# Linear attention's numerators computed transposed in strips of 512 tokens, with denominators written out 16-fold through DRAM, one-sided scaling of the queries' features, and half of the query tiles placed beside the keys

## The chip, the cores and the metric

The kernel runs on one core of one Trainium2 chip. The time is device time in microseconds (us) of one execution. Engines are named as in the profile: PE is TensorE (PEld its weight loads), DVE is VectorE, ACT is ScalarE, POOL is GpSimd, and SP is the engine that issues most of the DMAs.

## What is computed

One transformer block over 2048 tokens of width 512: a linear attention with 32 heads of 16 features, whose queries and keys go through a learned map and two softmaxes, then a mixture of 8 experts, all of them used for every token.

```python
def _A_ref(x, wqkv, w_phi, wo):                 # S = 2048, D = 512, H = 32, Dh = 16
    qkv = ... (x @ wqkv) ...
    pq = jnp.einsum("bhsd,hdf->bhsf", q, w_phi)
    pk = jnp.einsum("bhsd,hdf->bhsf", k, w_phi)
    phi_q = jnp.concatenate([_softmax(pq), _softmax(-pq)], axis=-1)
    phi_k = jnp.concatenate([_softmax(pk), _softmax(-pk)], axis=-1)
    kv = jnp.einsum("bhsf,bhsd->bhfd", phi_k, v)
    z  = jnp.einsum("bhsf->bhf", phi_k)
    num = jnp.einsum("bhqf,bhfd->bhqd", phi_q, kv)
    den = jnp.einsum("bhqf,bhf->bhq", phi_q, z)[..., None] + 1e-6
    o = num / den
    return ...(o)... @ wo
def _B_ref(x, wg, w1, w2):                      # E = 8, F = 1792, top 8 of 8
    h = _gelu(jnp.einsum("nd,edf->nef", xt, w1))
    y = jnp.einsum("nef,efd->ned", h, w2)
    out = jnp.einsum("ne,ned->nd", cw, y)       # cw: softmax of xt @ wg, renormalized
h = x + _A_ref(_layernorm(x), A_wqkv, A_w_phi, A_wo)
out = h + _B_ref(_layernorm(h), B_wg, B_w1, B_w2)
```

## The kernel before

The tokens are 16 tiles of 128; four tiles are a chunk of 512, two chunks a half. Every large product is made of three fast matmuls of 512 columns (`mm3`, lines 73 to 75), on operands that `split` (lines 62 and 63) has cut into a high part (a copy on ACT) and a low part (a subtraction on DVE). Matmuls on plain 32-bit data, as those of `k_sum`, `q_num` and `gate`, are issued as two instructions each.

**Attention.** For each tile of x: `x_norm`, `x_trans`, `x_low` make its transposed operand; `k_proj` makes keys and values; `k_exp` and `k_feat` make the keys' features; `k_sum` (line 264) adds 32 small products to `kvp`, a PSUM bank that is held through all keys and has, for each head, 32 features by 16 values plus one column of sums. When the last tile is in, `keys_done` spreads it into `kv` (line 307) with zeros where the heads don't match (`hmask`). Queries follow tile by tile: `q_proj`; `q_sub` (lines 202 and 203 on DVE, 282 and 283 on POOL); `q_exp` (line 287); `q_feat`, which is `feat_norm` (sums on line 209, reciprocals on 210, one product over all 1024 features on POOL, line 211); `q_trans` (eight 128x128 transposes, line 299, two copies by ACT, line 300); `q_num` (eight matmuls of 68 columns, line 319, that take the transposed features as stationary weights, then on DVE the denominator plus 1e-6 on 323, its reciprocal on 324, the quotient on 325, twice each); `q_otrans` (four transposes of the result, and its split); `q_out` (twelve fast matmuls with `wos`, the residual added on 338, the layer norm's statistics); `q_norm` (line 182), `q_ntrans` (line 189 and the copies on 355). For each chunk `gate` (line 370), `gate_norm` and `gate_rows` (lines 401 to 406) make the expert weights.

**Experts.** `moe` runs over experts and blocks of F for the first half of the tokens, then the second. `quad` makes seven products of six fast matmuls each (two-by-two block products with seven multiplications), `down` seven more, whose sums go to DRAM by accumulating DMAs on POOL's queue (line 602). `operands(0)` cuts the first half into seven operand blocks; `spill(1)` writes the second half's to DRAM, with `block_sums` making the differences on line 419.

**What sets the order.** `steps` calls the stages in the order of `STAGES`, each with a lag in steps; a scheduling layer then fixes one static order for each engine. Engines run their queue in order, so an instruction that waits holds up all behind it. PSUM has eight banks: four of the pool `ps`, four of `pacc` (one is `kvp` until the keys are done). Tiles in SBUF come from two pools with 43 and 15 slots, handed out in turn. Four of the 16 query projections stand ahead of the last `k_sum`; all other query work on PE comes behind it, and its end overlaps with the first quads.

## Time and profile before

| | before |
|---|---|
| median of 3 runs | 2330.6 us (2330.36 to 2331.09) |
| the profiled execution's own time | 2329.5 us |
| span of its profile | 2327.8 us |
| PE, DVE, ACT, POOL busy | 99%, 92%, 76%, 22% of the span |
| first matmul of a key projection | 13.39 us |
| last instruction of the last `k_sum` begins | about 133 us |
| first matmul of the experts (line 622) | 260.76 us |

The profile lists groups of instructions by source line, engine and tile names, with their count, their busy time and the mean duration of one. PE's instructions overlap in its pipeline, so a group's pace, the distance from one to the next, is less than the mean duration of one. In the view of stretches, the idle time of an engine is the length less its busy time; PEclk is the granted clock. Tiles of both SBUF pools are called s.

### The profile page before, as it was taken

The page shows a single profiled execution, that of the slowest core. Times are in us where ns is not written, and L with a number is a line of the kernel's source. Part 1 is how long each engine was busy: PE and PEld are TensorE (multiplying, and loading weights), DVE is VectorE, ACT ScalarE, POOL GpSimd, SP SyncE. Part 2 cuts the span into 40 slices and gives each one's busy share as a digit, 9 for nine tenths or more (in the row PEclk, how much of TensorE's full clock was granted, in tenths as well). Part 3 has the DMA queues.
Part 4 walks back from the last instruction along what each step waited for, and adds up shares of the span by engine and source line. Part 5 has one row for each costly group of instructions (what it writes and reads, how often), then busy time and mean ns, then how long its engine had stood idle before and what let it go on. Part 6 is the DMA issues. An engine that isn't in the chain of part 4 may idle for free.

```text
span 2327.8 us, 34005 instructions
## 1 busy us (share of the span) xinstructions
PE 2313.0 (99%) x12100; PEld 2021.0 (87%) x12100; DVE 2135.0 (92%) x3199; ACT 1762.7 (76%) x2933; POOL 520.0 (22%) x619
## 2 busy tenths in 40 slices
PE   9999999999999999999999999999999999999999
PEld 8888888888888888888888888888888888888887
DVE  7777899999999999999998999889999999999998
ACT  5444688787777878778777887777777778777774
POOL 5576201111111111111111331211111111111121
PEclk9999999999999999999999999999999999999999
DMA  3002458888888788887889898998888888878888
GB/s 129 24 6 74 139 175 179 165 159 164 166 165 168 152 175 153 179 163 147 175 155 222 180 207 165 215 208 171 160 166 159 168 165 158 174 150 178 164 162 188
DMA packets 173497, 370.92 MB, mean 159 GB/s; under 512 B 15216, under 2 KB 80368, under 8 KB 173296
## 3 DMA queue, kind: packets, MB, share of 16 engines
q0 software_dynamic: 63776, 210.79, 54.3%
q1 hardware_dynamic: 108224, 157.77, 21.3%
q8 instruction: 96, 1.57, 0.3%
q14 instruction: 73, 0.60, 0.1%
q10 hardware_dynamic: 1328, 0.18, 0.0%
HBM read 157.34 MB, written 220.79 MB: 162 GB/s over the span
## 4 chain that ended last, share of the span: by engine, by line
PE 75%; issue 5%; DVE 4%; ACT 1%; POOL 1%; DMA 1%; POOLq 0%; DVEq 0%; ACTq 0%
PE ps L73 13%; PE ps L74 13%; PE ps L75 13%; PE pacc L74 12%; PE pacc L75 12%; PE pacc L73 12%; DVE s L63 2%; POOL acc1m L602 1%; DVE s L612 1%; DMA acc1m<-s 1%; DVE s L561 1%; ACT s L62 1%; DVE s L550 0%; DMA h<-s 0%; DVE s L419 0%
## 5 line engine op out<-in xcount | busy, mean ns | idle before, releaser
L63 DVE TENSOR_TENSOR s<-s,s 128x512 fp32r<-128x512 f32 (+1 forms) x806 | 760.9, 957 | 85.9 <-ACT s L62 77.7
L62 ACT ACTIVATE s<-s 128x512 fp32r<-128x512 f32 (+1 forms) x806 | 675.4, 844 | 14.1 <-DVE s L561 6.0
L73 PE MATMUL pacc<-s,s 128*128 128x512 f32 x1728 | 657.8, 381 | 2.6 <-DVE s L63 1.7
L74 PE MATMUL pacc<-s,s 128*128 128x512 f32 x1728 | 655.3, 379 | 0.4 <-DVE s L63 0.4
L75 PE MATMUL pacc<-s,s 128*128 128x512 f32 x1728 | 654.9, 379 | 0.0
L73 PE MATMUL ps<-s,s 128*128 128x512 f32 x1664 | 634.2, 381 | 1.5 <-ACT ps L616 0.7
L74 PE MATMUL ps<-s,s 128*128 128x512 f32 x1664 | 631.8, 380 | 0.6 <-DVE s L63 0.6
L75 PE MATMUL ps<-s,s 128*128 128x512 f32 x1664 | 631.1, 379 | 0.0
L600 ACT ACTIVATE s<-pacc 128x512 f32<-128x512 f32 x756 | 441.4, 593 | 138.7 <-PE pacc L75 134.3
L611 ACT ACTIVATE ps<-ps 128x512 f32<-128x512 f32 x448 | 257.5, 585 | 171.6 <-DVE ps L663 116.1
L73 PEld LDWEIGHTS pacc<-s,s 128*128 128x128 f32 x1728 | 326.5, 189 | 50.5 <-DVE s L63 1.5
L74 PEld LDWEIGHTS pacc<-s,s 128*128 128x128 f32 x1728 | 326.6, 189 | 47.1 <-DVE s L63 1.5
L75 PEld LDWEIGHTS pacc<-s,s 128*128 128x128 f32 x1728 | 326.6, 189 | 46.2
L73 PEld LDWEIGHTS ps<-s,s 128*128 128x128 f32 x1664 | 314.8, 189 | 50.0 <-ACT ps L616 1.6
L74 PEld LDWEIGHTS ps<-s,s 128*128 128x128 f32 x1664 | 314.8, 189 | 44.9 <-DVE s L63 1.3
L75 PEld LDWEIGHTS ps<-s,s 128*128 128x128 f32 x1664 | 314.8, 189 | 44.5
L602 POOL DMA_DIRECT2D acc0m<-s x189 | 162.2, 858 | 810.6 <-ACT s L600 790.2
L612 DVE TENSOR_TENSOR s<-ps,s 128x512 f32<-128x512 f32 x448 | 302.5, 684 | 40.0 <-ACT ps L611 33.5
L602 POOL DMA_DIRECT2D acc1m<-s x175 | 149.7, 857 | 726.2 <-ACT s L600 706.1
L561 DVE TENSOR_TENSOR s<-s,s 128x1024 f32<-128x1024 f32 x224 | 272.1, 1216 | 0.1
L616 ACT ACTIVATE ps<-ps 128x512 f32<-128x512 f32 x226 | 133.3, 590 | 53.1 <-PE ps L75 52.3
L533 DVE TENSOR_TENSOR s<-s,s 128x1024 fp32r<-128x1024 f32 x111 | 134.8, 1214 | 0.0
(121 smaller groups left out, 1774.8 us busy)
## 6 DMA issues: line engine op xcount, KB each, us to landing
acc0m<-s POOLq DMA_DIRECT2D x196, 512.0 KB, 5.7
acc1m<-s POOLq DMA_DIRECT2D x184, 512.0 KB, 5.7
s<-in_B_w_dram SPq DMA_DIRECT2D x224, 256.0 KB
s<-in_B_w_dram SPq DMA_DIRECT2D x111, 512.0 KB
s<-in_A_x_dram SPq DMA_DIRECT2D x32, 256.0 KB
s<-cwT SPq DMA_DIRECT2D x16, 512.0 KB
h<-s SPq DMA_DIRECT2D x16, 256.0 KB
acc0m<-acc0m POOLq DMA_DIRECT2D x28, 128.0 KB, 7.6
```

Source lines behind the costliest of these rows:

```text
L62: nc.scalar.activation(hi, src, AF.Copy)
L63: return eng.tensor_tensor(lo, src, hi.bitcast(F32), op=ALU.subtract)
L73: nc.tensor.matmul(out_, al, bh, start=first, stop=False, skip_group_check=True)
L74: nc.tensor.matmul(out_, ah, bl, start=False, stop=False, skip_group_check=True)
L75: nc.tensor.matmul(out_, ah, bh, start=False, stop=last, skip_group_check=True)
L533: nc.vector.tensor_tensor(sl, s, sh.bitcast(F32), op=ALU.subtract)
L561: nc.vector.tensor_tensor(r, B[a], B[b], op=ALU.subtract)
L600: nc.scalar.activation(e[:, d], p[d], AF.Copy)
L602: return nc.gpsimd.dma_start(macc[h, m], e, accum_op=ALU.add)
L611: nc.scalar.activation(src, src, AF.Gelu_apprx_tanh)
L612: nc.vector.tensor_tensor(B[b][:, q % 2], src, CW[h, e][:, int(b[2]) - 1], op=ALU.mult)
L616: nc.scalar.activation(dst, src, AF.Copy)
```

## The change

Numerators are computed transposed: the stationary operand is now a small block of `kv` (64 features of two heads by 32 values), the moving one the transposed features of 128 tokens, and the result is a strip with features on partitions and 512 tokens in a row, so that no transposes of `o` are needed ahead of `q_out`. For each chunk `q_den` makes the 32 denominators of its 512 tokens in one bank, takes their reciprocals, writes each 16 times to DRAM (`rden`), and reads them back as two tiles in the shape of the strips; `q_num` multiplies. `wo` is loaded with its rows in the strips' order (`load_wo`, 16 DMAs). `q_feat` leaves the first softmax unscaled and multiplies the second by the ratio of both sums, since a common factor of numerator and denominator drops out (1e-6 is added to the first softmax's rows of z). The differences of `spill` go to POOL. Stages are now listed with the steps at which their tiles run: query tiles 0 to 7 go beside the keys from step 6 on, 8 to 15 behind them; `q_out`, `q_norm` and `q_ntrans` run in pairs of tiles from step 22 on.

```diff
-    hmask = consts.tile([P, HG], F32, name="hmask")
...
+    rden = [dram.tile([H, Dh, TC, P], F32, name=f"rden{c}") for c in range(NT // TC)]
...
     def q_feat(t):
-        st["qf", t] = feat_norm(st.pop(("qe", t)))
+        e = st["qf", t] = st.pop(("qe", t))
+        s = work.tile([P, H, 2], F32, name="s")
+        nc.vector.tensor_reduce(s..., e..., axis=AX.X, op=ALU.add)
+        nc.vector.reciprocal(s[:, :, 1], s[:, :, 1])
+        nc.vector.tensor_tensor(s[:, :, 1], s[:, :, 0], s[:, :, 1], op=ALU.mult)
+        nc.gpsimd.tensor_tensor(e[:, :, 1, :], e[:, :, 1, :], s[:, :, 1:2].to_broadcast([P, H, Dh]), op=ALU.mult)
...
     def keys_done():
-        for g in range(NG):
-            nc.vector.tensor_tensor(kv[:, g, :]..., kvp[...]..., hmask..., op=ALU.mult)
+        for j in range(HG):
+            ...
+            nc.vector.tensor_scalar(z[r, a:...:H + 2], v[r, :, Dh], eps[r], None, op0=ALU.add)
+            nc.scalar.activation(kvn[r, :, e, :], v[r, :, :Dh], AF.Copy)
+    def q_den(c):
+        p = ps()
+        for g in range(NG):
+            for j in range(TC):
+                nc.tensor.matmul(p[j * H:(j + 1) * H, :P], zs[:, g, :], st["ph", c * TC + j][:, g, :],
+                                 start=(g == 0), stop=(g == NG - 1), skip_group_check=True)
+        d = work.tile([P, P], F32, name="den", bufs=1)
+        nc.vector.reciprocal(d, p[:, :P])
+        for j in range(TC):
+            nc.sync.dma_start(rden[c][:, :, j, :],
+                              d[j * H:(j + 1) * H].rearrange("h (o t) -> h o t", o=1).to_broadcast([H, Dh, P]))
+        for a in range(2):
+            r = st["d", c, a] = s4([P, 2, 512])
+            nc.sync.dma_start(r, rden[c][...]...)
-    def q_num(t):
+    def q_num(c):
-                nc.tensor.matmul(p[:, i * HN:(i + 1) * HN], phT[:, b * n + i, :], kv[:, b * n + i, :],
-                                 start=True, stop=True)
-            nc.vector.tensor_scalar(den, nv[:, :, Dh:], 1e-6, None, op0=ALU.add)
-            nc.vector.reciprocal(den, den)
-            nc.vector.tensor_tensor(o[...]..., nv[:, :, :Dh], den.to_broadcast([P, H // 2, Dh]), op=ALU.mult)
-    def q_otrans(t):
-        p = transposed(st.pop(("o", t)), ps_acc())
-        split(o[:, 0], o[:, 1], p)
+        for l in range(2):
+            p = [ps() for _ in range(2)]
+            for j in range(TC):
+                for g in range(KD):
+                    for a in range(2):
+                        r = slice(a * 2 * F2, (a + 1) * 2 * F2)
+                        nc.tensor.matmul(p[a][g * F2:(g + 1) * F2, j * P:(j + 1) * P], kvn[r, l * KD + g]...,
+                                         ph[j][r, l * KD + g, :], start=True, stop=True, skip_group_check=True)
+            for a in range(2):
+                r = st["d", c, a][:, l]
+                nc.vector.tensor_tensor(r, p[a], r, op=ALU.mult)
+                o = st["O", c, 2 * a + l] = s4([P, 2, 512], F32R)
+                split(o[:, 0], o[:, 1], r)
...
-        return block_sums(h, lambda b, src: nc.sync.dma_start(later[h, b], src))
+        return block_sums(h, lambda b, src: nc.sync.dma_start(later[h, b], src), nc.gpsimd)
...
+    BO = 22
+    early = [6 + t for t in range(8)]
+    STAGES = [..., (q_num, listed([21, 22, 25, 27])), ..., (q_den, listed([19, 20, 23, 25])),
+              (q_out, pairs(BO)), ...,
+              (q_proj, queries(0, [17, 17, 18, 18, 19, 19, 20, 20])), ...]
```

Three places show what the scheduler made of it. The first is PE in the middle of the query stage, one tile's numerators before, whose weights are the tile's transposed features (s_2184) and whose moving operand is kv (s_120):

```order
L75 MATMUL ps<-s_752,s_1165 128x512
L189 MATMUL pacc<-ident,s_2097 128x128 x4
L319 MATMUL ps<-s_120,s_2184 128x68 x8
L299 MATMUL pacc<-ident,s_2064 128x128 x8
L73 MATMUL pacc<-s_1889,s_2158 128x512
```

Now, at the numerators of chunk 0 (tiles s_1613 to s_1939 are transposed features, s_127 holds kv and z), with the transposes of tile 8 (line 312) and the numerators of chunk 1 (s_2004 to s_2285) right behind:

```order
L355 MATMUL ps<-s_1735,s_127 32x128 x4
L355 MATMUL ps<-s_1613,s_127 32x128 x4
L355 MATMUL ps<-s_1735,s_127 32x128 x4
L355 MATMUL ps<-s_1837,s_127 32x128 x8
L355 MATMUL ps<-s_1939,s_127 32x128 x8
L312 MATMUL ps<-ident,s_2178 128x128 x8
L355 MATMUL ps<-s_2004,s_127 32x128 x4
L355 MATMUL ps<-s_2092,s_127 32x128 x4
L355 MATMUL ps<-s_2181,s_127 32x128
L355 MATMUL ps<-s_2004,s_127 32x128 x4
```

Eight matmuls of a tile have become 64 of a chunk, which fill all four ps banks, and the transposes behind them need one of these banks again. The second place is DVE there. Before, a query tile's quotient stood among that tile's own work:

```order
L323 TENSOR_SCALAR den<-ps 128x16
L63 TENSOR_TENSOR s_2158<-pacc,s_2158 128x512
L324 RECIPROCAL den<-den 128x16
L323 TENSOR_SCALAR den<-ps 128x16
L325 TENSOR_TENSOR s_2165<-ps,den 128x256
L324 RECIPROCAL den<-den 128x16
L325 TENSOR_TENSOR s_2165<-ps,den 128x256
```

Now the first product with chunk 0's reciprocals (line 361, s_2233) stands behind the sums of two later tiles' features (line 300) and chunk 1's reciprocals (line 338):

```order
L300 TENSOR_REDUCE s<-s_2271 128x64
L300 TENSOR_REDUCE s<-s_2277 128x64
L338 RECIPROCAL den<-ps 128x128
L301 RECIPROCAL s<-s 128x32 x2
L302 TENSOR_TENSOR s<-s 128x32
L361 TENSOR_TENSOR s_2233<-ps,s_2233 128x512
L302 TENSOR_TENSOR s<-s 128x32
L361 TENSOR_TENSOR s_2235<-ps,s_2235 128x512
L361 TENSOR_TENSOR s_2233<-ps,s_2233 128x512
L361 TENSOR_TENSOR s_2235<-ps,s_2235 128x512
```

The quotient has moved behind work of other tiles. The third place is where the experts begin. Before, PE went from a query tile's output projection to one transposed tile, the priming matmuls of line 622 and the first product; DVE had made that product's low part (s_3005) among the query work:

```order
L324 RECIPROCAL den<-den 128x16
L392 RECIPROCAL gr<-gr 128x4
L325 TENSOR_TENSOR s_2927<-ps,den 128x256
L393 TENSOR_TENSOR cw<-gate,gr 128x4x8
L63 TENSOR_TENSOR s_3005<-s_2504,s_3004 128x1024
L338 TENSOR_TENSOR s_2791<-pacc,s_2791 128x512
```

Now DVE goes from the residual of tile 11 (s_3009) through the first expert weights (lines 546 to 563, the old 516 to 533) to chunk 3's four strips (s_3067 and s_3069), with the first product's low part (s_3245) among them:

```order
L187 TENSOR_SCALAR mb<-mv 128x1
L546 TENSOR_TENSOR s_3227<-s_2917 128x256
L548 TENSOR_TENSOR s_3227<-s_2917 128x256
L547 TENSOR_TENSOR s_3227<-s_3227,s_2917 128x256
L549 TENSOR_TENSOR s_3227<-s_2917,s_3227 128x256
L556 TENSOR_TENSOR s_3232<-s_2917,s_3232 128x512
L361 TENSOR_TENSOR s_3067<-ps,s_3067 128x512
L563 TENSOR_TENSOR s_3241<-s_3227,s_3240 128x1024
L361 TENSOR_TENSOR s_3069<-ps,s_3069 128x512
L63 TENSOR_TENSOR s_3245<-s_2906,s_3244 128x1024
L361 TENSOR_TENSOR s_3067<-ps,s_3067 128x512
L63 TENSOR_TENSOR s_3283<-s_3067,s_3283 128x512
```

and PE, from the last matmul of tile 11's output projection to the first of tile 12's (which reads s_3283), has little between:

```order
L75 MATMUL pacc<-s_2084,s_3000 128x512
L201 MATMUL pacc<-ident,s_3129 128x128 x4
L201 MATMUL pacc<-ident,s_3131 128x128 x4
L431 MATMUL pacc<-ident,cw 128x128
L652 MATMUL ps<-s_3244,s_3232 128x512 x2
L73 MATMUL ps<-s_3244,s_3232 128x512
L74 MATMUL ps<-s_3245,s_3232 128x512
L75 MATMUL ps<-s_3244,s_3232 128x512
L73 MATMUL pacc<-s_1798,s_3283 128x512
```

More of the change, by code (lines that the diff above doesn't have):

```diff
@@ new lines, in block_kernel, with keys_done @@
+    kz = s2([P, 2, NG, H])
+    nc.gpsimd.memset(kz, 0.0)
+    kvn, zs = kz[:, 0].rearrange("p g (e d) -> p g e d", e=2), kz[:, 1]
+    def keys_done():
+        v = kvp[:, :NG * DE].rearrange("p (g d) -> p g d", g=NG)
+        z = zs.rearrange("p g h -> p (g h)")
+        for j in range(HG):
+            s_, e = divmod(j, 2)
+            r = slice(j * F2, (j + 1) * F2)
+            a = s_ * (H // 2) + e
+            nc.vector.tensor_scalar(z[r, a:a + (NG - 1) * (H + 2) + 1:H + 2], v[r, :, Dh], eps[r], None, op0=ALU.add)
+            nc.scalar.activation(kvn[r, :, e, :], v[r, :, :Dh], AF.Copy)
@@ L337, in q_out @@
+    def q_out(t):
+        c, j = divmod(t, TC)
+        p = ps_acc()
+        for k in range(KD):
+            o = st["O", c, k]
+            mm3(p, (o[:, 0, j * P:(j + 1) * P], o[:, 1, j * P:(j + 1) * P]), wos[k], k == 0, k == KD - 1)
+            if j == TC - 1:
+                del st["O", c, k]
         r = st["h", t] = st.pop(("r", t))
@@ L989, in block_kernel @@
     wv = split_all(raw_v)
-    steps(0, 32 + NT, NT, STAGES, hook)
+    steps(0, BO + 14, STAGES, hook)
     for _ in late["m"]:
```

141 lines of the change are left out of this document (73 added, 68 removed).

## Prediction

> **What bounds the kernel now.** I read the page first: how busy each engine is, and the slices.
>
> ```profile
> span 2327.8 us, 34005 instructions
> ...
> PE 2313.0 (99%) x12100; PEld 2021.0 (87%) x12100; DVE 2135.0 (92%) x3199; ACT 1762.7 (76%) x2933; POOL 520.0 (22%) x619
> ```
>
> A busy share of 99% says only that PE nearly always has an instruction in flight. Whether it runs at its pace is seen from the starts of its matmuls, in the timeline of PE, in which two fast matmuls that are 20 apart stand here:
>
> ```profile
> 20.39 0.38 PE L73 MATMUL pacc<-s,s 128*128 128x512 f32 x1
> ...
> 24.70 0.38 PE L75 MATMUL pacc<-s,s 128*128 128x512 f32 x1
> ```
>
> (24.70 - 20.39) / 20 gives 0.216 us each. The view of stretches then shows where PE lost time: the keys (13.39 to 113.69 us), the queries, the start of the experts, and a piece of their steady run.
>
> ```profile
> 13.39:113.69 100.30, 100.13 (x1236) 86.35 (x1234) 82.66 (x150) 53.35 (x83) 56.46 (x69) 1.00 0.14 46
> 113.69:260.76 147.07, 142.52 (x1177) 127.50 (x1176) 119.54 (x286) 74.49 (x127) 88.29 (x81) 0.99 0.19 57
> 260.76:340.72 79.96, 77.87 (x421) 64.44 (x419) 73.90 (x134) 63.95 (x113) 7.49 (x16) 1.00 0.47 167
> 460.00:1000.00 540.00, 540.00 (x2504) 472.86 (x2503) 505.93 (x716) 429.58 (x717) 88.95 (x105) 1.00 0.83 165
> ```
>
> The columns are length, PE, PEld, DVE, ACT, POOL, granted clock, DMA share, GB/s. In the steady run PE is never idle: nothing there is touched, and no later wait can absorb a gain. So what the change takes out of PE's queue before about 340 us comes off the end, and each new wait of PE there goes on top. PE idled 147.07 - 142.52 = 4.6 us beside the queries and 2.1 us at the experts' start, where DVE was busy 73.9 of 80 us. There is one more loss:
>
> ```profile
> 152.60 1.08 PE L319 MATMUL ps<-s,s 128*128 128x68 f32 x8 [1.49 <-DVE s L325]
> ...
> 155.32 0.63 PE L74 MATMUL ps<-s,s 128*128 128x512 f32 x1
> 155.75 0.63 PE L75 MATMUL ps<-s,s 128*128 128x512 f32 x1
> ...
> 150.00:155.00 5.00, 3.50 (x25) 3.40 (x26) 4.96 (x12) 3.04 (x5) 3.47 (x3) 0.89 0.02 3
> 155.00:160.00 5.00, 5.00 (x26) 4.32 (x26) 5.00 (x12) 2.74 (x4) 3.42 (x3) 0.77 0.00 0
> ```
>
> After an idle 1.49 us the clock falls: fast matmuls are 0.43 us apart, half speed. From the means 0.89 and 0.77 of two stretches of 5 us, (0.11 + 0.23) x 5 x 2 = 3.4 us ran so, which costs 1.7 us. Idle and clock together are 8.4 us.
>
> **What goes from PE.** In the timeline, a query tile's old numerators and the transposes of its result:
>
> ```profile
> 172.54 0.60 PE L189 MATMUL pacc<-ident,s 128*128 128x128 f32 x4
> 172.98 1.90 PE L319 MATMUL ps<-s,s 128*128 128x68 f32 x16
> 174.72 1.04 PE L299 MATMUL pacc<-ident,s 128*128 128x128 f32 x8
> ```
>
> From start to start the transposes take 0.44 us and the 16 instructions 1.74 us (0.109 each). Over 16 tiles that is 7.0 + 27.8 = 34.8 us. The eight transposes of the features stay.
>
> **What is added on PE.** A chunk's denominators are 32 matmuls, so 64 instructions, in the form of the expert gate: 32 columns of weights, 128 moving, four column groups in turn. Its timeline:
>
> ```profile
> 227.78 1.30 PE L370 MATMUL pacc<-s,wg_raw 128*32 128x128 f32 x32
> 229.00 0.66 PE L189 MATMUL pacc<-ident,s 128*128 128x128 f32 x4
> 229.49 0.30 PE L380 MATMUL pacc<-ident,gT 128*128 128x128 f32 x1
> ```
>
> 1.22 us for 32, or 0.038 each: 2.44 us a chunk, 9.8 us in all. The numerators are 64 matmuls (128 instructions) a chunk, 512 in all, of 64 partitions by 32 columns. No row has that form. If the two row halves also run side by side, each costs half a gate's, 0.019 (9.8 us); if they don't, 0.038 (19.7 us); if nothing overlaps, line 319's 0.109 (55.8 us). I take 0.0235, 12 us, near the lower end, because consecutive matmuls alternate between the halves and between two banks. The Trainium skill, TensorE: Matmul & The Clock Gate, Part 3 on packing, has three column tiles at 2.38-fold and three by three at 6.32-fold; my estimate by that ratio for two row halves is 11 us, one less in the sum; no run here shows it. So PE's work falls by 34.8 - 9.8 - 12 = 13.0 us (bounds 15.2 and 5.3, without overlap a rise of 30.8).
>
> Packed groups also cost at their edges: the transposes behind the gate take 0.49 us to the next start, not 0.44. A dozen new groups with two edges each are 1.2 us; I take 1.5 (0 to 3).
>
> **What moves.** Eight projections (2.6 us each) and most transposes of early tiles now stand among the keys. PE's sum doesn't change by that, as long as the other engines keep up. The first stretch holds 15 key tiles: 6.7 us of PE a step, 9.3 with a projection; DVE 82.66 / 15 = 5.5, POOL 3.8. A query tile adds, from these rows:
>
> ```profile
> L209 DVE TENSOR_REDUCE s<-s 128x64 f32<-128x1024 f32 x32 | 38.8, 1213 | 22.6 <-ACT s L254 22.0 <-ACT s L287 0.7
> L202 DVE TENSOR_REDUCE mx<-s 128x32 f32<-128x512 f32 x32 | 21.3, 665 | 20.3 <-POOL s L283 20.3
> L210 DVE RECIPROCAL s<-s 128x64 f32<-128x64 f32 x32 | 17.5, 546 | 0.3
> L211 POOL TENSOR_TENSOR s<-s,s 128x1024 f32<-128x1024 f32 x32 | 63.0, 1968 | 69.7 <-DVE s L210 36.0 <-DVE mb L175 21.2 <-DVE den L323 5.6
> L282 POOL TENSOR_TENSOR s<-s,mx 128x512 f32<-128x512 f32 x16 | 18.3, 1143 | 0.0
> ```
>
> on DVE 1.2 for the sums, two extrema at 0.67 and about 0.4 for half the reciprocals and the ratio, so 2.9, which makes 8.4 of 9.3; on POOL two subtractions (2.3) and half of line 211 (1.0), in all 7.1. Both fit: PE hides them at no cost; if waits between the two engines use that slack up, I price it at 0.3 us for each of eight steps, 2.4 us. POOL also takes the four spill differences (8 us at line 211's size); behind them on its queue stand only the first accumulating DMAs, which wait for ACT anyway, and on SP the weight loads two quads ahead.
>
> **The denominators' round trip.** A chunk is 1 MB out in 2048 pieces of 512 bytes, then 1 MB back. SP must wait for the write before it issues the read. The nearest landings:
>
> ```profile
> acc0m<-s POOLq DMA_DIRECT2D x196, 512.0 KB, 5.7
> q1 hardware_dynamic: 108224, 157.77, 21.3%
> ```
>
> Two transfers at 5.7 us give 11.4. From the second row a packet takes 21.3% of 16 x 2327.8 us / 108224 = 73 ns, so 2048 over 16 engines would take 9.3 us, and by bytes 3.3; the trip lies between some 8 and 18 us. I take 11.5. The matmuls of the numerators don't wait for it, only DVE's product, and the next user of the PSUM bank.
>
> **New waits of PE**, by the order shown ahead.
> (a) The first denominators stand 0.8 us of transposes behind the last `k_sum`, and need DVE's four additions: 1 us.
> (b) Rows for ACT's copies and exponentials:
>
> ```profile
> L300 ACT ACTIVATE s<-pacc 128x512 f32<-128x512 f32 x32 | 17.9, 597 | 9.6 <-PE pacc L299 9.6
> L287 ACT ACTIVATE s<-s 128x1024 f32<-128x1024 f32 x16 | 16.9, 1058 | 40.4 <-POOL s L283 40.4
> ```
>
> Chunk 0's product stands on DVE behind tile 10's sums, whose exponentials stand on ACT behind the copy of the last early-issued projection. From that projection's end: ACT 0.6 + 1.2 + 2.1 (copies, two exponentials of 1.06), DVE 1.2 (sums), 1.1 (128 reciprocals, twice line 210), 0.6 (small ones) and 0.7 (product), so 7.5 us until a bank is free. PE has 29 denominators' matmuls (2.2 us) and 48 to 64 numerators' (about 3 us) until then, and waits 2 to 3; again 1 to 2 for the following banks. Chunk 1 repeats it behind its round trip and eight POOL subtractions of 1.14 us: 3 to 5. Of 6 to 10, I take 6.
> (c) Chunk 3. The durations:
>
> ```profile
> L338 DVE TENSOR_TENSOR s<-pacc,s 128x512 f32<-128x512 f32 x16 | 10.9, 682 | 0.3 <-PE pacc L75 0.2
> L172 DVE BATCH_NORM_STATS2 bn<-s 128x6 f32<-128x512 f32 x32 | 21.4, 670 | 3.8 <-DMA s<-in_A_x_dram 3.8
> L533 DVE TENSOR_TENSOR s<-s,s 128x1024 fp32r<-128x1024 f32 x111 | 134.8, 1214 | 0.0
> L516 DVE TENSOR_TENSOR s<-s 128x256 f32<-128x256 f32 x111 | 46.1, 415 | 0.0
> L63 DVE TENSOR_TENSOR s<-s,s 128x1024 fp32r<-128x1024 f32 x406 | 496.1, 1222 | 77.4 <-ACT s L62 72.7
> ```
>
> From tile 11's last matmul DVE has a residual and statistics (0.7 + 0.7 + 0.4), the weights' sums (4 x 0.42 + 0.7), three products (2.1), two long operations (2.4) and one short (0.7): 9.4 us, or 8.3 at the spacing of a busy DVE. PE has 2.1 us to do meanwhile: about 6 us idle, and 1.5 more until the fourth strip is split. I take 7. After so long a wait I count one clock drop, 1.7. The Trainium skill, TensorE: Matmul & The Clock Gate, Part 1, lets the clock fall only after an idle window of about 3.4 us; the trace shows half speed after 1.49 us, so the trace decides, and (b) can drop the clock too. By that rule the sum is as it stands, by the trace up to 1.7 more.
> Chunk 2 has some 20 us of PE work beside its trip: nothing.
> Sum of new waits 1 + 6 + 7 + 1.7 = 15.7, in place of the old 8.4.
>
> **DVE's relief.**
>
> ```profile
> L325 DVE TENSOR_TENSOR s<-ps,den 128x256 f32<-128x256 f32 x32 | 13.1, 418 | 0.3
> L324 DVE RECIPROCAL den<-den 128x16 f32<-128x16 f32 x32 | 7.3, 237 | 0.0
> L323 DVE TENSOR_SCALAR den<-ps 128x16 f32<-128x16 f32 x32 | 4.2, 137 | 0.0
> ```
>
> The tile's quotient leaves (twice 0.14 + 0.24 + 0.42, 1.6 us), a product of 0.68 comes, and four long differences go to POOL; where the experts start, DVE bounds PE, so I give back 1.5 of the 2.1 us idle there.
>
> **Sum.** -13.0 + 1.5 + 15.7 - 8.4 - 1.5 = -5.7 us against the profiled execution's 2329.5 (span 2327.8 and 1.7 around it): 2323.8. The median shown is 1.1 higher than that execution, so 2325 us.
>
> **Rivals.**
> - *Same*: the waits eat it. With (b) at 10, (c) at 8 and a second clock drop, the sum is +1 us, 2332. For it: (c) follows from a fixed order, DVE can't be earlier. Against: DVE loses 16 x 0.9 us of work in all. Chance 0.28, with all that falls within 0.2% (4.7 us, about what this kernel's measurement can tell from no change).
> - *Slower, by packing*: the row halves don't overlap. The point from which it decides is 0.035 us for one of the 512 instructions (17.7 us, no gain left), and from 0.044 it is slower by over 0.2%; at 0.109 the time is 2325 + 44 = 2369. For it: no row shows the form. Against: the gate's instructions, in four column groups, start 0.038 us apart, a third of line 319's distance. Chance 0.06.
> - *Slower, by the trip*: at 18 us a round trip chunk 1's product waits 6.5 us more and chunk 3's 5, for PE too: 2336. It decides from 13 to 14 us, where the trip outlasts DVE's own queue. Chance 0.16.
> - *Larger gain*: 0.019 each and waits (b) of 3 us only: 2325 - 2 - 3 = 2320, without the clock drop and (c) at 5, 2316. It is part of faster.
> - *It doesn't do what it says*: the waits only move into the keys, because POOL and DVE there, at 76 and 90%, lag behind: + 2.4 us, inside same.
>
> **Numbers.** Forecast: faster, 0.50 (2308 to 2326). Same 0.28, slower 0.22. The range from 2309 to 2338 leaves out the unpacked case and a little at the fast end.
>
> **What would show it.** Right: the group of line 355 on PE 10 to 14 us busy, that of line 335 about 10; no transposes of `o`; PE idle some 7 us between the last output projection of chunk 2 and the first of chunk 3, released by DVE line 63; idle of transposes on line 312 released by DVE line 361; the steady run unchanged. Wrong: line 355 above 20 us, DVE waits on DMA ahead of line 361, idle PE among the keys, or a steady run with another pace.

## The result: 23.5 us slower

| | median, us | ratio to before | 95% interval |
|---|---|---|---|
| before (4 runs of this comparison) | 2330.7 | 1 | |
| changed | 2354.2 | 1.0103 | 1.0085 to 1.0120 |

The forecast was 2325 us, and the range ended at 2338. The profiled execution of the changed kernel has a span of 2354.3 us, 26.5 more than before's.

The page of the changed kernel, and then its view of stretches, with the columns and the four stretches of the prediction:

```profile
span 2354.3 us, 34893 instructions
...
PE 2311.7 (98%) x12548; PEld 2008.0 (85%) x12548; DVE 2133.1 (91%) x3131; ACT 1766.9 (75%) x2937; POOL 515.0 (22%) x627
```

```profile
13.39:113.69 100.30, 100.14 (x1111) 86.16 (x1110) 80.88 (x158) 57.48 (x86) 63.90 (x77) 1.00 0.14 46
113.69:260.76 147.07, 126.58 (x1702) 105.43 (x1700) 104.75 (x198) 66.83 (x117) 63.95 (x72) 0.96 0.38 115
260.76:340.72 79.96, 67.07 (x346) 52.52 (x347) 65.50 (x114) 53.05 (x95) 15.97 (x15) 0.85 0.37 126
460.00:1000.00 540.00, 540.00 (x2504) 472.86 (x2503) 505.37 (x716) 428.63 (x715) 89.69 (x105) 1.00 0.80 164
```

The keys and the steady run are as they were: PE has no idle time there. All of the loss lies between 113.69 and 340.72 us. There PE idled 20.5 + 12.9 = 33.4 us, against 4.6 + 2.1 = 6.7 before. The clock column went from 0.99 and 1.00 to 0.96 and 0.85; (1 - clock) x length gives 5.9 + 12.0 = 17.9 us at most (some of it falls on idle time), against 1.5 by the same reckoning before. Idle time alone is 26.7 us more, as much as the span grew. PE's busy time is nearly the same (2311.7 us, 2313.0 before): what PE has less to do and what the lower clock costs it about cancel.

Where PE waited, by the view of its waits over the whole run (who waited on what for whom; sum in us, times, longest):

```profile
PE ps L335 <- DVE s L328: 5.5, 1, 5.5
PE ps L73 <- ACT ps L646: 4.4, 2, 3.9
PE ps L652 <- DVE s L563: 4.2, 1, 4.2
PE pacc L431 <- DVE cw L427: 3.9, 2, 3.6
PE pacc L73 <- DVE s L63: 3.6, 3, 2.0
PE ps L312 <- DVE s L361: 3.5, 2, 3.0
PE ps L73 <- DVE s L563: 1.8, 1, 1.8
...
PE pacc L407 <- ACT s L395: 1.3, 1, 1.3
PE ps L355 <- DVE den L338: 1.2, 1, 1.2
PE ps L73 <- DVE s L361: 0.9, 1, 0.9
...
PE ps L335 <- DVE s L361: 0.7, 1, 0.7
PE ps L73 <- ACT s L284: 0.7, 1, 0.7
PE ps L355 <- ACT s L284: 0.7, 1, 0.7
```

No single wait does it. The forecast's places are there (lines 335, 63, 312 and 355; line 652 is the experts' first product, which stands ahead of chunk 3's projections), and so is one for which a gain was forecast: lines 646, 431 and 407 and the wait of line 73 for line 563 belong to the experts' start. Of line 63's 3.6 us, 3.0 (two waits) lie in these stretches.

The first row in the timeline of PE, with what follows it:

```profile
164.75 3.64 PE L335 MATMUL ps<-s,s 128*32 128x128 f32 x64 [5.50 <-DVE s L328]
168.32 0.80 PE L73 MATMUL ps<-s,s 128*128 128x512 f32 x1
168.91 0.63 PE L74 MATMUL ps<-s,s 128*128 128x512 f32 x1
169.34 0.43 PE L75 MATMUL ps<-s,s 128*128 128x512 f32 x1
```

After 5.5 us without work the 64 instructions take 3.57 us to the next start, and fast matmuls are 0.43 us apart (169.34 - 168.91): half speed again, after this wait as after the 1.49 us of the kernel before. It does not follow every wait, though. In the same timeline:

```profile
194.33 0.48 PE L73 MATMUL pacc<-s,s 128*128 128x512 f32 x1 [2.01 <-DVE s L63]
194.65 0.38 PE L74 MATMUL pacc<-s,s 128*128 128x512 f32 x1
194.87 0.38 PE L75 MATMUL pacc<-s,s 128*128 128x512 f32 x1
```

After an idle 2.01 us, longer than 1.49, these start 0.22 us apart, at full speed. So the length of one wait doesn't settle it, and what does these runs don't show.

### The profile page after: what moved, and what is told of

The parts are those of the page before. It is cut to its first block, busy times and chain, and to the rows that moved or that the text cites. A ratio compares the mean times of both kernels' runs of the same rounds, so it can differ in the third digit from the quotient of the medians.

```text
span 2354.3 us, 34893 instructions
## 1 busy us (share of the span) xinstructions
PE 2311.7 (98%) x12548; PEld 2008.0 (85%) x12548; DVE 2133.1 (91%) x3131; ACT 1766.9 (75%) x2937; POOL 515.0 (22%) x627
## 4 chain that ended last, share of the span: by engine, by line
PE 83%; issue 6%; DVE 5%; DMA 2%; POOL 2%; ACT 2%; SPq 0%; POOLq 0%; DVEq 0%; ACTq 0%
PE pacc L73 14%; PE pacc L74 14%; PE pacc L75 14%; PE ps L73 13%; PE ps L74 13%; PE ps L75 13%; DVE s L63 2%; POOL acc1m L632 1%; DMA h<-s 1%; ACT s L62 1%; DVE s L580 0%; DVE s L591 0%; DMA acc1m<-s 0%; DVE s L642 0%; DVE s L300 0%
## 5 line engine op out<-in xcount | busy, mean ns | idle before, releaser
L63 DVE TENSOR_TENSOR s<-s,s 128x1024 fp32r<-128x1024 f32 (+1 forms) x822 | 773.7, 955 | 93.7 <-ACT s L62 83.9
L62 ACT ACTIVATE s<-s 128x1024 fp32r<-128x1024 f32 (+1 forms) x822 | 684.9, 839 | 21.8 <-DVE s L361 8.9
```

Of the source, the lines that this page charges most:

```text
L62: nc.scalar.activation(hi, src, AF.Copy)
L63: return eng.tensor_tensor(lo, src, hi.bitcast(F32), op=ALU.subtract)
```

## Experiments

Four theories stood at first. **A**: the schedule took away the query work that covered PE's waits. **E**: the denominators' trip through memory sets the waits. **C**: the packed matmuls themselves pull the clock down. **D**: POOL's differences hold DVE up. **F**, the order in the engines' queues, came in after the first four runs. (Some expectations use the letter A, or B, for the reading that stands against the one under test; each says which.) In each diff lines of the changed kernel carry a minus, unless something else is said, and `...` stands for lines left out. e4, e12 and e15 leave out the division by the denominators: they show what costs time and do not compute the block.

| run | what | median, us | ratio, 95% interval |
|---|---|---|---|
| e1_old_order | new arithmetic, old schedule (output side two steps later) | 2360.5 | 1.0131 (1.0115 to 1.0146) |
| e2_fill | idle matmuls in PE's waits | 2357.6 | 1.0117 (1.0100 to 1.0134) |
| e3_spill_dve | differences on DVE | 2350.2 | 1.0086 (1.0071 to 1.0101) |
| e4_no_trip | product reads rows of x | 2336.5 | 1.0028 (1.0017 to 1.0038) |
| e5_order_exp | exponentials ahead on ACT | 2347.5 | 1.0076 (1.0059 to 1.0093) |
| e6_read16 | written once, read 16-fold | 2343.2 | 1.0058 (1.0043 to 1.0073) |
| e7_last_sum_first | last key sums ahead | 2350.3 | 1.0087 (1.0072 to 1.0102) |
| e8_all_four | e3, e5, e6, e7 together, one transfer for the write | 2338.4 | 1.0032 (1.0020 to 1.0044) |
| e9_fill_half | e2 with half the matmuls | 2350.7 | 1.0087 (1.0070 to 1.0103) |
| b1_scaling | before + one-sided scaling | 2324.4 | 0.9975 (0.9965 to 0.9985) |
| b2_spill_pool | before + differences on POOL | 2336.7 | 1.0028 (1.0018 to 1.0038) |
| b3_scaling_early | b1 + the changed schedule | 2334.1 | 1.0018 (1.0008 to 1.0027) |
| e10_old_order_short | e1 + short trip, e3 | 2338.5 | 1.0036 (1.0023 to 1.0049) |
| e11_old_order_step | e10 + one step of slack | 2339.8 | 1.0039 (1.0024 to 1.0054) |
| e12_no_trip_repaired | e4 + e7, e3 | 2326.6 | 0.9983 (0.9974 to 0.9992) |
| e13_spread_pe | PE spreads, no trip, e7, e3 | 2342.1 | 1.0050 (1.0035 to 1.0065) |
| e14_spread_old_order | e13's spread on old schedule | 2340.6 | 1.0046 (1.0029 to 1.0063) |
| e15_no_trip_late_exp | e4 + the changed order on ACT | 2341.6 | 1.0049 (1.0032 to 1.0066) |

### e1: the new arithmetic on the schedule of before

```diff
...
-              (q_trans, queries(7, [21, 22, 22, 23, 23, 24, 24, 25])), (q_den, listed([19, 20, 23, 25])),
...
+    STAGES = [(q_exp, lag(19)), (k_proj, lag(1)), (x_norm, lag(-2)), (q_feat, lag(19)), (q_num, chunk(25)),
+              (q_norm, lag(28)), (x_trans, lag(-1)), (x_low, lag(-1)), (k_sum, lag(3)), (q_trans, lag(20)),
+              (q_den, chunk(23)), (q_sub, lag(17)), (q_out, lag(26)), (gate, chunk(33)), (q_ntrans, lag(29)),
...
```

(`lag(n)` is one tile a step, `chunk(n)` one chunk every four steps.)

> The changed kernel's arithmetic (strips, 16-fold denominators, one-sided scaling, differences on POOL) on the schedule of before: no query tile beside the keys, one query tile a step behind them, a chunk's denominators three steps and its numerators five steps behind its first tile's transposes, output projections one tile a step and two steps later than before. Theory A (the schedule took the work away that covered PE's waits; the arithmetic is sound): PE has about 14 us less work than before and idles 5 to 12 us up to 340 us, so 2316 to 2326 us, faster than before. Rival B (the arithmetic itself, by the trip through memory, its waits or a low clock under packed matmuls, costs the 24 us): 2345 to 2360, as the changed kernel.

Measured 2360.5 us: theory A as it stood is not borne out, since the old schedule doesn't bring the gain back (POOL's differences are still in it, too). Its trace shows the trip's length. The queue of SP (the write's issue, and the issue of the read behind it), then DVE's timeline at the product:

```profile
164.58 3.90 SPq L340 DMA_DIRECT2D rden<-den  x4
...
172.18 0.90 SPq L345 DMA_DIRECT2D s<-rden  x2
```

```profile
178.76 0.69 DVE L361 TENSOR_TENSOR s<-ps,s 128x512 f32<-128x512 f32 x1 [3.91 <-DMA s<-rden]
```

From 164.58 to 178.76 it takes 14.2 us until DVE has the data: 7.6 to the read's issue (of which SP issues for 3.9) and 6.6 for the read. Here DVE does wait for it, 3.91 us. The prediction took 11.5, and let the trip outlast DVE's own queue from 13 or 14.

### e2 and e9: filling PE's waits

```diff
     def q_den(c):
         p = ps()
+        if c == 0:
+            fill(p, 46)
```

`fill(p, n)` makes n matmuls of the identity with itself; likewise 34 stand ahead of the experts' first product and 28 ahead of the third chunk's gate rows. e9 has 23, 17 and 14.

> The changed kernel with idle matmuls of the identity put on PE where it waited longest: 46 ahead of the first denominators (5.5 us idle), 34 ahead of the experts' first product (4.2 and 0.9), 28 ahead of the third chunk's gate rows (3.6). They fill the waits and change no wait of another engine. Theory A (part of the loss is the clock that falls behind an idle PE): the spells at half clock behind these places (6.8, 10.2 and 6.8 us, worth up to 11.9 us) go, 2342 to 2348 us. Rival C (the clock falls under the packed matmuls and the mixed work, not behind idleness): the spells stay, 2353 to 2358.

> As e2_fill with half as many idle matmuls (23, 17, 14): each turned out to be two instructions of 0.11 us, so that e2_fill's ran up to twice as long as the waits and set PE back by some 11 us. Theory A2 (the clock that falls behind an idle wait costs time): the spells behind these three places go and nothing is set back, 2342 to 2348 us. Theory F (PE runs from wait to wait there; what it loses by the clock it would wait for anyway): 2352 to 2356.

e2's matmuls are two instructions each, which I had not counted, so they ran twice as long as the waits: 2357.6 us. e9 has the intended length. Its timeline of PE at the first place:

```profile
160.56 5.40 PE L334 MATMUL ps<-ident 128*128 128x128 f32 x46 [0.53 <-ACT s L284]
165.89 1.96 PE L342 MATMUL ps<-s,s 128*32 128x128 f32 x64
```

The 64 denominators' instructions now take 1.96 us, not 3.64. So the half speed of this group goes when the idle time ahead of it is filled, and packed matmuls run at full speed: theory C falls. But e9 gains only 3.5 us, less than A2's 6 to 12 and more than the 2 at most of F. At the second place PE still waited 3.1 us ahead of the filling, so not every spell is gone: the clocks of the two stretches are 0.98 and 0.92, which is 9.3 us at most where the changed kernel has 17.9. About half of the clock's part is gone, and less than half of that comes off the end, as PE then meets other waits (4.0 us for line 572, 3.6 for line 655, the 563 and 646 of the changed kernel). The idle matmuls also show how little PE's work decides at these places: e9 gave PE 2 x 54 = 108 more instructions (5.40 / 46 = 0.117 us each, 12.7 us together) and the kernel became 3.5 us faster; e2 gave it twice that, some 25 us, and lost 3.4. **Work put into PE's waits is nearly free.** I read from it that work taken from PE just ahead of such a wait brings next to nothing.

### e3, b2: POOL's differences

```diff
-        return block_sums(h, lambda b, src: nc.sync.dma_start(later[h, b], src), nc.gpsimd)
+        return block_sums(h, lambda b, src: nc.sync.dma_start(later[h, b], src))
```

> The changed kernel with the four differences of the second half back on DVE (one word). Theory A (order of the experts' start, not POOL, makes PE wait): 2352 to 2357 us, since four operations of 1.2 us come back to a busy DVE. Rival D (POOL's long differences, 2.6 us each, slow DVE down at the experts' start and hold the stores): PE's 3.9 and 1.8 us idle at 319 to 325 us and the half clock behind them go, 2340 to 2348.

> The kernel before with the four differences of the second half on POOL, and nothing else of the change. Theory D (DVE's operations with both operands in SBUF stand still while POOL runs one of these; 2.7 us each in place of 0.7): 2333 to 2338 us. If it only hurts together with the shifted start of the experts: 2329 to 2331.

Back on DVE: 4.0 us less. Alone on top of before: 6.4 more. b2 lies in theory D's range, e3 between both. The mechanism, in the changed kernel's timelines of POOL and of DVE at the experts' start:

```profile
300.35 3.15 POOL L449 TENSOR_TENSOR s<-s,s 128x1024 f32<-128x1024 f32 x1 [13.20 <-ACT s L395]
304.45 2.36 POOL L449 TENSOR_TENSOR s<-s,s 128x1024 f32<-128x1024 f32 x1 [0.96 <-PE pacc L407]
```

```profile
301.20 0.68 DVE L642 TENSOR_TENSOR s<-ps,s 128x512 f32<-128x512 f32 x1
301.80 1.97 DVE L546 TENSOR_TENSOR s<-s 128x256 f32<-128x256 f32 x1
303.70 0.41 DVE L548 TENSOR_TENSOR s<-s 128x256 f32<-128x256 f32 x1
...
304.48 2.61 DVE L549 TENSOR_TENSOR s<-s,s 128x256 f32<-128x256 f32 x1
```

Lines 546, 548 and 549 are operations of the same size on SBUF alone. With POOL free one takes 0.41 us; while POOL's difference runs it ends 0.3 us after POOL does (301.80 + 1.97 against 300.35 + 3.15, and 304.48 + 2.61 against 304.45 + 2.36). Line 642, which has an operand in PSUM, is not held (0.68). The Trainium skill, SBUF — State Buffer, section Who interferes with whom, says that VectorE and GpSimd contend for one pair of ports, and that the second to come waits until the first has finished; its section SBUF: two separate sides counts a VectorE operation with two inputs in SBUF among these. The trace agrees, with 2.61 us in place of 0.41.

### e4, e5, e15: the trip and the order of ACT's queue

```diff
-            v = rden[c][a * (H // 2):(a + 1) * (H // 2)]
-            nc.sync.dma_start(r, v.rearrange("(l h) o j t -> (h o) l (j t)", l=2))
+            i = c * TC * P + a * 2 * P
+            nc.sync.dma_start(r, x[i:i + 2 * P, :].rearrange("(l p) d -> p l d", l=2))
```

> The changed kernel in which the denominators are written as before but DVE's product reads rows of x in their place, so that the read waits for no write (leaves out the division). Theory A (the in-order queues of DVE, ACT and POOL set the waits, the data lay there 5 us ahead of chunk 0's product): 2350 to 2355 us. Rival E (the trip of 7.6 us sets the waits of chunks 0, 1 and 3): the waits by line 361 (3.0, 0.9, 0.7 us) and the half clock behind them go, 2338 to 2346.

2336.5 us, 17.7 less, more than rival E asked for. But the trace shows that something else moved too. In the changed kernel the queue of POOL, of ACT and of DVE (the last row is the reciprocal of chunk 1's denominators):

```profile
165.39 1.07 POOL L290 TENSOR_TENSOR s<-mx,s 128x512 f32<-128x512 f32 x1
```

```profile
171.75 0.60 ACT L284 ACTIVATE s<-ps 128x512 f32<-128x512 f32 x1 [6.75 <-PE ps L75]
174.34 0.60 ACT L284 ACTIVATE s<-ps 128x512 f32<-128x512 f32 x1 [1.99 <-PE ps L75]
178.35 0.60 ACT L284 ACTIVATE s<-ps 128x512 f32<-128x512 f32 x1 [3.41 <-PE ps L75]
181.89 0.60 ACT L284 ACTIVATE s<-ps 128x512 f32<-128x512 f32 x1 [2.95 <-PE ps L75]
...
183.34 2.01 ACT L294 ACTIVATE s<-s 128x1024 f32<-128x1024 f32 x2
```

```profile
184.45 2.35 DVE L300 TENSOR_REDUCE s<-s 128x64 f32<-128x1024 f32 x2 [10.72 <-ACT s L294]
186.71 0.95 DVE L338 RECIPROCAL den<-ps 128x128 f32<-128x128 f32 x1
```

POOL had the arguments of two exponentials ready at 166.5 us. They ran at 183.3, behind four copies of later projections, for each of which ACT waited on PE; DVE stood behind them for 10.7 us, and chunk 1's denominators behind DVE. In e4 the static order came out other. Its timeline of ACT:

```profile
165.88 1.06 ACT L294 ACTIVATE s<-s 128x1024 f32<-128x1024 f32 x1
167.36 1.06 ACT L294 ACTIVATE s<-s 128x1024 f32<-128x1024 f32 x1 [0.42 <-POOL s L290]
172.63 0.60 ACT L284 ACTIVATE s<-ps 128x512 f32<-128x512 f32 x1 [4.21 <-PE ps L75]
```

So e4 takes away two things. e5 takes the second alone; the added edge says only that the copy of tile 12 stands behind the exponentials of tiles 9 and 10:

```diff
-        nc.scalar.activation(e, e, AF.Exp)
+        i = nc.scalar.activation(e, e, AF.Exp)
+        if t in (9, 10):
+            tc.add_manual_dep(st["qc", 12].ins, i.ins.name, mybir.DependencyInfo(
+                mybir.DependencyClass.NoSync, mybir.DependencyReason.DATA), reason="order")
```

> The changed kernel with one constraint on ACT's order: the exponentials of query tiles 9 and 10 stand ahead of the copies of the projections of tiles 12 to 15 (in the changed kernel they were ready at 166.5 us and ran at 183.3, behind four copies that wait for PE one after the other). The trip of the denominators stays. Theory F (the order of the engines' queues, which came out other when the trip was taken away, held the second chunk's denominators and all behind them back): the sums at 184.5 and the denominators of chunk 1 at 187.7 us come 9 to 15 us earlier, 2338 to 2346 us. Rival E (the trip as such, 14 us from the write's issue to the data): 2350 to 2355.

6.7 us less, above theory F's range and below E's: chunk 1's reciprocals run at 179.3 instead of 186.7, and chunk 3's first product still runs 6.0 us earlier (252.8 instead of 258.8). e15 has the opposite edge on top of e4: `i.ins` stands behind `st["qc", 15].ins`, the copy of tile 15.

> e4_no_trip (rows of x in the place of the denominators, which leaves out the division) with the changed kernel's order on ACT: the exponentials of tiles 9 and 10 stand behind the copies of tiles 12 to 15. With e5 it completes a square of two causes, trip and order. If both cost by themselves: 2336.5 + 6.7 = 2342 to 2345 us. If the order alone made e4's gain: 2350 to 2355. If the trip alone: 2335 to 2338.

2341.6 us, just under the 2342 to 2345 of "both cost by themselves". The square:

| | changed order on ACT | exponentials ahead |
|---|---|---|
| with the denominators | 2354.2 | 2347.5 (e5) |
| rows of x in their place | 2341.6 (e15) | 2336.5 (e4) |

**The order of one queue, which no line of the change states, costs 5.1 to 6.7 us** in either row: F holds; within a row DVE's order stays much the same. The product's dependence on the denominators costs 11.0 to 12.6 in either column, and the two add up. But that dependence is more than the trip. e4 and e15 take away the whole chain ahead of the product (32 matmuls, the reciprocals, write and read), and the build orders DVE otherwise without it: e15's runs chunk 3's first product at 243.8 us, ahead of the first expert weights (line 566, 250.4), the changed kernel's at 258.8, between them. And in the changed kernel no product waits for the data; by its group's row (line and form: busy us, mean ns, idle before) the only idle time ahead of line 361 is 0.8 us, for PE:

```profile
L361 DVE TENSOR_TENSOR s<-ps,s 128x512 f32<-128x512 f32 x16 | 10.6, 680 | 0.8 <-PE ps L355 0.8
```

So E's number came, and its mechanism, a wait for the trip, is not seen there. On the old schedule DVE does wait for the read (5.5 us in e1, 3.7 in e10, 6.0 in e11), on the new one only in e6, 0.5. How the 11.0 to 12.6 divide between the trip's length and the order built around it stays open.

### e6, e7, e8: a short trip, the last sums first, and all four

```diff
-        for j in range(TC):
-            nc.sync.dma_start(rden[c][:, :, j, :],
-                              d[j * H:(j + 1) * H].rearrange("h (o t) -> h o t", o=1).to_broadcast([H, Dh, P]))
+        for j in range(TC):
+            nc.sync.dma_start(rden[c][:, j, :], d[j * H:(j + 1) * H])
...
+                nc.sync.dma_start(r[:, l], v[l * n:(l + 1) * n].rearrange("h (o j) t -> h o (j t)", o=1)
+                                  .to_broadcast([n, Dh, TC * P]))
```

> The changed kernel with the denominators written once (64 KB a chunk, 128 pieces) and spread on the read: the read of 1 MB takes each row 16 times. The trip falls from 14.2 us (write's issue at 169.4, data at some 183.6) by the write's 1024 pieces less, to an estimated 9 to 10. Rival E (the trip sets the waits): 2340 to 2348 us, and the data of the later chunks come 4 to 5 us earlier. Theory F (the order of the queues does): 2350 to 2356.

2343.2 us, inside E's range. Its order on ACT also moved (the exponentials ran at 175.8 us, behind two copies and not four), so the 11.0 us aren't the shorter trip's alone.

```diff
-    STAGES = [(k_proj, tile_by_tile(1)), (x_norm, tile_by_tile(-2)),
+    STAGES = [(k_sum, {NT + 2: (NT - 1,)}), (k_proj, tile_by_tile(1)), (x_norm, tile_by_tile(-2)),
...
-              (q_proj, queries(0, [17, 17, 18, 18, 19, 19, 20, 20])), (k_sum, tile_by_tile(3)),
+              (q_proj, queries(0, [17, 17, 18, 18, 19, 19, 20, 20])), (k_sum, {t + 3: (t,) for t in range(NT - 1)}),
```

> The changed kernel with the last key tile's sums and the additions behind them put at the head of step 18, ahead of two projections and two tiles' transposes. Every theory: PE has some 6 us of work between the last sum and the first denominators, and the 5.5 us idle at 158 us and the 6.8 us at half clock behind it go (up to 8.9 us). If that gain comes through to the end: 2344 to 2348. If PE only meets the next wait sooner (line 361's at 188 to 203 us, which hang on ACT's exponentials): 2350 to 2354.

2350.3 us: the 5.5 us wait is gone, but the last sums themselves now wait 2.8 us for POOL's scaling of their features, and 3.9 us come through of up to 8.9. That is the second range: PE mostly meets its next wait sooner.

> The changed kernel with four repairs together: the exponentials' order (alone 6.7 us less), denominators written once in one transfer and spread on the read (alone 11.0), the last key sums first (alone 3.9), the second half's differences back on DVE (alone 4.0). If the four act at places of their own: 2354 - 25.6 = 2328 to 2330 us, and with one issue of the write in place of four, 2 us less a trip, down to 2325. If the order and the trip are the same wait seen twice (both hold chunk 1 back): the larger of the two counts, 2335 to 2338.

2338.4 us: 15.8 us for the four, not 25.6. Part of that is that e6 had moved the order on ACT already, so that e5's gain is at least in part in e6's; the rest these runs don't assign. With all four the kernel is still slower than before, though PE has some 14 us less to do.

### b1 and b3: the change's parts that need no strips

b1 is the kernel before with the new `q_feat` alone; b3 adds the changed `STAGES` and hooks, with the old `q_num` and `q_otrans` in pairs at steps 20 and 21.

> The kernel before with the queries' features scaled on one side only, and nothing else of the change. By the rows, POOL's product falls from 1.97 to 1.14 us a tile and DVE has 0.3 less and 0.5 more: PE isn't held by either there, 2328 to 2331 us. If the extra ratio sits in the chain to the transposes: up to 2334.

> b1_scaling with the changed kernel's schedule: eight query tiles beside the keys, the others and the output side in pairs, the same steps; numerators, division and transposes stay those of before, so no trip and POOL without the differences. If the crowded schedule costs of itself: 2334 to 2345 us. If it is sound, and the trip and the chunk's work cost: 2320 to 2327, as b1_scaling or a little better.

b1 gives 2324.4 us, **the fastest kernel of this study**, 5.8 less than before, and better than the 2328 to 2331 that stood. b3 gives 2334.1: the schedule costs 9.6 us on top of b1. The second and third stretch of b1, then those of b3:

```profile
113.69:260.76 147.07, 145.24 (x1201) 130.21 (x1200) 122.90 (x311) 79.42 (x137) 74.17 (x82) 1.00 0.20 59
260.76:340.72 79.96, 78.35 (x422) 65.75 (x421) 74.24 (x134) 64.07 (x113) 8.17 (x16) 1.00 0.51 174
```

```profile
113.69:260.76 147.07, 146.13 (x1369) 131.96 (x1359) 118.56 (x301) 74.38 (x130) 64.30 (x75) 1.00 0.19 62
260.76:340.72 79.96, 72.26 (x381) 59.06 (x380) 70.85 (x125) 62.12 (x107) 6.99 (x14) 0.98 0.46 161
```

In b1 PE's idle time beside the queries falls from 4.6 to 1.8 us, and the clock stays up, with POOL's busy time there down from 88.3 to 74.2 us (which wait of PE hung on which of POOL's products I didn't follow up). In b3 PE is even fuller beside the queries (0.9 us idle), and then idles 7.7 us at the experts' start (b1: 1.6), with DVE idle there too. So the early tiles do fit beside the keys. I read the loss as theory A at one place: the schedule leaves too little query work for the time when the first quads wait for gates, sums and splits. That is not shown by itself, since b3 has the early tiles and the output side in pairs at once.

### e10 to e14: what is left of the trip

e10 is e1 with e6's read, a single write and e3; e11 has one more step between transposes, denominators and numerators.

> e1_old_order (strips and one-sided scaling on the schedule of before) with the denominators written once in one transfer, spread on the read, and the differences back on DVE. In e1_old_order line 361 waited 5.5 us for the trip's data and held PE's banks 14 us in all. If the change's arithmetic is sound and only the trip, POOL's differences and the crowded schedule cost: 2322 to 2330 us. If taking a chunk of four tiles at once costs of itself (PE waits for a chunk's last tile whatever the schedule): 2335 to 2342, as e8_all_four.

> As e10_old_order_short, with one more step between a chunk's last transposes, its denominators and its numerators, so that every wait of PE for a chunk has some 9 us more of other tiles' work beside it. If waits on a chunk's data are what is left: 2314 to 2322 us (PE has 14 us less work than before, and the scaling's 6 us are part of that). If the chunk's work stands in the way of DVE at the experts' start in any order: within 3 us of e10_old_order_short.

2338.5 and 2339.8 us: the repairs help by 22 us, but the old schedule doesn't beat the repaired new one, and slack in steps brings nothing. Both fall where "a chunk of four tiles costs of itself" stood.

> e4_no_trip (rows of x in the place of the denominators, which leaves out the division) with the last key sums first (3.9 us alone) and the differences on DVE (4.0 alone). It shows what the strips cost without any trip. If these repairs add up: 2328 to 2330 us. If PE only meets other waits (the chunk's products and splits on DVE, the experts' start): 2333 to 2337, near e8_all_four, and the trip, once shortened, is no longer what costs.

2326.6 us: the two repairs give 9.9 on top of e4, and e8, with a short trip, is 11.8 above. Even without the denominators, then, strips and schedule together are 2.1 us slower than b1. e13 has no trip either and computes everything: PE multiplies a 32 x 128 selection (ones where a row's head is the column's) with a tile's 32 rows of denominators, and ACT copies the result from PSUM.

```diff
+        p = [ps_acc() for _ in range(TC)]
+        for k in range(KD):
+            for j in range(TC):
+                b = slice(j * H, (j + 1) * H)
+                nc.tensor.matmul(p[j][:, k * P:(k + 1) * P], sel[b, k * P:(k + 1) * P], d[b], start=True, stop=True,
+                                 skip_group_check=True)
+        for j in range(TC):
+            for a in range(2):
+                nc.scalar.activation(r[a][:, :, j * P:(j + 1) * P],
+                                     p[j][:, 2 * a * P:2 * (a + 1) * P].rearrange("p (l t) -> p l t", l=2), AF.Copy)
```

> The changed kernel without a trip and with the whole computation: PE spreads the denominators, 16 matmuls a chunk of a 32 x 128 selection against the 32 rows of a tile's denominators, four row groups into four banks, and ACT copies them to the layout that DVE's product reads; the last key sums first and the differences on DVE, as in e12_no_trip_repaired. PE gains 32 instructions a chunk, 3.5 us in all if the four row groups run side by side (0.027 each), 14 us if they don't (0.109). If the trip is what e8_all_four lost against e12 (12 us): 2328 to 2333 us. If PE's wait for the copies takes its place: 2337 to 2345.

> The same spreading by PE on the schedule of before (as e10_old_order_short, no trip, differences on DVE). If the trip was what kept e10 and e11 at 2338 to 2340 us: 2315 to 2325, the fastest so far, since this schedule costs some 10 us less than the changed one (b3 against b1). If chunks of four tiles cost by themselves there: 2332 to 2340.

2342.1 and 2340.6 us: no better than with the short trip (e8, 2338.4), so the trip through memory alone is not what e12 saves. e14 lies just above its second range, "chunks of four tiles cost by themselves". The second and third stretch of e12, and then of e13:

```profile
113.69:260.76 147.07, 140.35 (x1850) 118.28 (x1849) 121.72 (x238) 83.76 (x148) 67.22 (x78) 1.00 0.43 128
260.76:340.72 79.96, 71.92 (x342) 59.12 (x342) 69.79 (x119) 60.84 (x105) 7.06 (x12) 0.96 0.47 155
```

```profile
113.69:260.76 147.07, 134.56 (x1912) 113.60 (x1912) 109.48 (x201) 81.25 (x158) 63.39 (x70) 0.97 0.18 57
260.76:340.72 79.96, 70.59 (x399) 57.42 (x398) 68.56 (x133) 58.54 (x102) 10.21 (x18) 0.96 0.44 156
```

At the experts' start both lose alike (8.0 and 9.4 us idle, as b3 does). Beside the queries e12 idles 6.7 us at full clock, e13 12.5 at 0.97. What e12 alone has is a product whose second operand waits for no denominators. In e13 it waits for a longer chain on the engines themselves (16 more matmuls, as 32 instructions, and 8 more copies a chunk), and the kernel is 3.7 us slower than with the short trip. How much of e13's 12.5 us is that chain, how much the work in chunks of four tiles, and how much the orders that its queues took, these runs don't separate.

## Why the prediction was wrong

**Right.** PE's work: line 355's group and line 335's have these rows (by line and form: busy us, mean ns, idle before):

```profile
L355 PE MATMUL ps<-s,s 64*32 64x128 f32 x512 | 10.3, 273 | 1.9 <-DVE den L338 1.2 <-ACT s L284 0.7
L335 PE MATMUL ps<-s,s 128*32 128x128 f32 x256 | 10.3, 311 | 6.2 <-DVE s L328 5.5 <-DVE s L361 0.7
```

10.3 us each, where 12 and 9.8 were taken: the row halves do run side by side (10.3 / 512 = 0.020 us), and PE's work falls by 34.8 - 10.3 - 10.3 = 14.2 us, where 13.0 stood. The keys take the early projections at no cost. The steady run is unchanged. (b) came in size: the rows of lines 361, 63, 338 and 284 give 3.5 + 0.7 + 3.0 + 1.2 + 1.4 = 9.8 us, at the upper end of 6 to 10, of which 6 was taken. Only 4.2 of it has the releaser that was named, line 361. (c) has 4.2 + 0.9 = 5.1 us of 7, but PE waited there for the experts' first weights (line 563) ahead of chunk 3's projections, not, as the signs said, for the strips' split (line 63). None of the four signs of being wrong came.

**The step that failed** is the sum of the waits, "1 + 6 + 7 + 1.7 = 15.7, in place of the old 8.4", with "DVE's relief" of 1.5 behind it. The idle time in it is 1 + 6 + 7 - 1.5 = 12.5 us; PE idled 33.4. Term by term:

- *(a), "1 us"*: 5.5. I counted the four additions' time and not their place in DVE's queue, behind a tile's sums (line 300, at 159.3 us) that waited 3.2 us for ACT, which waited for POOL; between the additions DVE waits for ACT's copies, too, and the last begins at 164.45. e7, which puts other work of PE there, takes the wait away.
- *"DVE's relief", minus 1.5*: the experts' start idles 12.0 us (12.9 less the 0.9 of (c)), not 0.6: this is the largest miss of the waits. Two causes are shown. The differences on POOL hold DVE up (e3: 4.0; b2: 6.4), where the prediction looked only at who stands behind them on POOL's queue. And the schedule costs 9.6 us by itself (b3), with 7.7 us idle at that place. The sum also takes this place twice: the old 8.4 that goes out already holds all of the 2.1 us, and 1.5 of them go again. With 0.6 left in their place the sum is -3.6 and the forecast 2327.
- *"one clock drop, 1.7"*: the clock took up to 17.9 us from PE. One drop was counted, where nine waits are over 1 us. Nor is "half speed after 1.49 us" a rule: 2.01 us left the clock at full, 2.98 us and more did not. Little of it reaches the end, though: with about half of it gone, e9 gains 3.5 us.
- *The trip, "11.5"*: 14.2 us in e1, just past the 13 to 14 from which the rival decides. That rival was priced at 11 us for a trip of 18, so for 14.2 at next to nothing, and its sign, DVE waiting on DMA ahead of line 361, did not come in the changed kernel. That the square shows 11.0 to 12.6 for the dependence on the denominators is luck of the number; what the prediction had no term for is that the build orders DVE around that dependence.
- *The order on ACT* stood in (b), and its chain was read rightly: from the last projection's copy (181.89) to the transposes that take the bank (190.05) it is some 8.2 us, where 7.5 stood. But only PE's wait for the bank was priced, 2 to 3 us; e5 shows 6.7 for the whole, since all that follows comes later as well.
- *The one-sided scaling, priced at nothing on PE*: by itself it is worth 5.8 us (b1).

Behind the terms stands, as I read them, one error of method. The sum charged PE's work at full price in a stage that, once lighter, PE no longer bounds. In the kernel before, 142.5 of 147 us were PE's, and from "never idle" I concluded that work taken away comes off the end. That holds only as far as the next chain: DVE, ACT and POOL pass each tile on in turn, each queue in a fixed order, and in e9 12.7 us more work on PE, put into its waits, cost nothing.

By parts: scaling -5.8 (b1), schedule +9.6 (b3 less b1), strips, denominators and differences on POOL +20.1 (changed less b3); the sum is 23.9 against 2330.2 to 2330.4 in those runs. Taken singly from the changed kernel, the dependence on the denominators is worth 11 to 13, the order on ACT 5 to 7, the place of the last sums 3.9 (e7) and POOL's differences 4.0 (e3). That is more than 20.1: they overlap (e8), and PE's saving may stand against them, so they aren't shares of it.

## What to carry to other kernels

A saving on the engine that bounds counts only up to the next chain's length: before booking it, take the lighter engine's time in that stage and ask whether the other engines can hand work on that fast, in the order of their queues. Price each new dependency from the finished producer's place in its queue, not from its own duration, and expect a build that orders queues by itself to move work that the change doesn't touch. Try the parts of a change alone: here the smallest one was the gain.

## What the runs showed of the hardware

That POOL stops DVE's operations on SBUF alone, and not those with an operand in PSUM, was not expected at this size. Small matmuls pack well in fp32: 64 x 32 blocks in two row halves at 0.020 us an instruction, and in e13 32 x 128 blocks in four row groups, each into its own bank, by this row of its timeline at 1.17 / 32 = 0.037 us, a third of the 0.109 that line 319 took for 128 rows and half as many columns moved:

```profile
176.68 1.17 PE L341 MATMUL pacc<-den,s 32*128 32x128 f32 x32
```
